# A fused attention and two-layer mixture kernel: a table of shifts on the due values of 426 planned tasks

## The chip, the core and the metric

The kernel runs on one core of one Trainium2 chip. A core has five engines, each with a queue of its own that runs in order: TensorE (PE in the rows) multiplies matrices, VectorE (DVE) and ScalarE (ACT) work on rows of up to 128 partitions, GpSimd (POOL) does a part of the elementwise work and the scattered writes, and SyncE (SP) starts most of the DMAs. An instruction that needs the result of another engine waits on a semaphore, and all that is queued behind it on its engine waits too. The metric is the device time of one launch in microseconds (us).

## The reference

```python
# 1. attention: 4 batches, 8 heads, 576 positions, 64 wide
scores = scale * np.matmul(q, k.transpose(0, 1, 3, 2))
mask = (rel >= 0) & (rel < 128)
scores = np.where(mask, scores + bias[None], -1000000000.0)
attn = np.exp(scores - np.max(scores, axis=-1, keepdims=True))
attn = attn / (np.sum(attn, axis=-1, keepdims=True) + 1e-09)
x = np.matmul(attn, v)              # to (2304 tokens, 512)
# 2. a dense layer
h = x @ w_in                        # 512 -> 2048
x = (h - np.tanh(h)) @ w_out        # 2048 -> 512
# 3. each token goes to the one best of 8 experts
logits = xn @ en.T / tau            # xn, en: normalised rows
expert_idx = np.argmax(logits, axis=1)
for e in range(8):
    h = np.maximum(x[mask] @ w1[e], 0.0)
    out[mask] = gate_w[mask, None] * (h @ w2[e])
```

All of it is in fp32. The kernel keeps that precision by splitting an operand into a high and a low part and adding three products (hi·hi, hi·lo, lo·hi); that is why one logical product is three matmuls, and why so many small casts and subtractions (`hi`, `lo`) go before each.

## The kernel before

The 2304 tokens are 18 blocks of 128 (`b`), and 9 groups of two blocks (`g`). The attention of a block goes in four quarters of two heads each (`quarter`, L479): scores on TensorE (L507 in the first four blocks, which are computed in plain fp32 on 64 of the array's rows per head, `jj` 0 on the upper half and 1 on the lower; L513 in the later blocks), bias and minimum on VectorE (`soft`, L520 to L535), the exponential on ScalarE (L549), a transpose (in the first blocks on TensorE, L570, with its copy out at L574), and the product with v (L584, later L595). `x_out` (L678) turns the block and splits it into `xT` (its low part at L700 on VectorE).

The dense layer goes in 72 steps `p`, eight for each group (`step`, L753): two groups of twelve matmuls into a bank `h` (L769; the bank alternates with `p % 2`), then tanh on ScalarE (L774), `h - tanh` on VectorE (L777), the split `gh` (ScalarE, L782) and `gl` (VectorE, L786), then four groups of three matmuls each that add to `acc` (L793). The 32 pieces of weight of this layer are loaded and split once, in the first 80 us, by `weight` (L338): `top`, `rest`, `hi`, `lo` (L354 to L366), on VectorE and ScalarE. `route` picks the expert of each token and scatters the rows into buckets (L951). Then follow eight experts with room for 384, 320, 320, 288, 288, 288, 288 and 256 tokens: `g1` (L1243) to a bank `he`, relu and split (L1259 on ScalarE, L1265 on VectorE), `g2` (L1278) to `y`, one tile of 128 tokens for each `t`, then a scale by the gate (L1299) and an indirect DMA from GpSimd that puts the rows into the result (L1303).

No engine's queue is written out by hand. Each piece of work is a task: `add` (L92) notes the engines that may do it with a cost in us on each, a `due` value (roughly the step in which it is wanted), and what it reads and writes. There are 3449 tasks, 969 of them TensorE's. `order` (L111) is a list scheduler over these costs: of all tasks that are ready it takes again and again the one with the least `(start, due, number)`, and gives it to the engine on which it ends first. `build` (L1398) then emits the tasks in that order, and each engine's queue is the tasks that it got. `due` thus decides between tasks that could start at the same planned time; and since VectorE or ScalarE, or VectorE or GpSimd, may do some of them, it decides the engine too.

Of the kernel before, what the change touches and what calls it, by code (L numbers as in the profile page):

```python
# [78 lines left out]
SPLIT = [i for i in range(NB) if (i * 128) % S > S - 128]  # L79


class Plan:


# [24 lines left out]
        self.tasks.append((eng, fn, due, deps, take, free, late, port, lag))  # L109

    def order(self, places):  # L111
        T = self.tasks
        nd = [len(t[3]) for t in T]
        out = [[] for _ in T]
        for n, t in enumerate(T):
            for d in t[3]:
                out[d].append(n)
        ready = [0.0] * len(T)
        free = {}
        pipe, pool = 0.0, (0.0, 0.0)  # L120
        avail = {p: [0.0] * c for p, c in places.items()}
        cand = [n for n in range(len(T)) if nd[n] == 0]
        res = []
        while cand:
            best = None
            now = min(max(ready[n], min(free.get(e, 0.0) for e in T[n][0])) for n in cand)
            load = {}
            for n in cand:
                eng = T[n][0]
                if len(eng) == 1 and ready[n] <= now + 1.0:  # L130
                    e, = eng
                    load[e] = load.get(e, 0.0) + eng[e]
            for n in cand:
# [10 lines left out]
                e = min(fin, key=fin.get)  # L144
# [1529 lines left out]
```

## Time and profile before

| | |
|---|---|
| median of 3 runs | 772.67 us (771.83 to 773.18) |
| profiled execution | 773.24 us, its span (first to last instruction) 771.4 us |
| granted TensorE clock, share of full speed | 0.999 |
| busy: TensorE, VectorE, ScalarE, GpSimd | 754.1, 547.3, 444.1, 324.1 us |
| share of the span | 98%, 71%, 58%, 42% |

The time that lies around the span is 773.24 - 771.4 = 1.84 us. A row of a timeline gives the start, the duration and the instruction with its line, out<-in, and how many instructions it joins; in brackets stands how long the engine was idle before it and what released it. Matmuls run in a pipeline, so the durations of two that follow one another overlap, and the price of a group is better read from one start to the next. A table of stretches gives the busy time of PE, PE's weight loads, DVE, ACT and POOL inside each stretch, with the instructions in brackets.

### The profile page before, as it was taken

The page shows a single profiled execution, that of the slowest core. Times are in us where ns is not written, and L with a number is a line of the kernel's source. Part 1 is how long each engine was busy: PE and PEld are TensorE (multiplying, and loading weights), DVE is VectorE, ACT ScalarE, POOL GpSimd, SP SyncE. Part 2 cuts the span into 40 slices and gives each one's busy share as a digit, 9 for nine tenths or more (in the row PEclk, how much of TensorE's full clock was granted, in tenths as well). Part 3 has the DMA queues.
Part 4 walks back from the last instruction along what each step waited for, and adds up shares of the span by engine and source line. Part 5 has one row for each costly group of instructions (what it writes and reads, how often), then busy time and mean ns, then how long its engine had stood idle before and what let it go on. Part 6 is the DMA issues. An engine that isn't in the chain of part 4 may idle for free.

```text
span 771.4 us, 15217 instructions
## 1 busy us (share of the span) xinstructions
PE 754.1 (98%) x5165; PEld 669.3 (87%) x5165; DVE 547.3 (71%) x1492; ACT 444.1 (58%) x1001; POOL 324.1 (42%) x340
## 2 busy tenths in 40 slices
PE   8999999999999999999999999999999999999996
PEld 5878899898989998999998998989889898898895
DVE  5789989878786778776787774787537786676420
ACT  5778876565666574675764743666245565565321
POOL 0052335867773465367474612412203531431211
PEclk9999999999999999999999999999999999999999
DMA  9994369947564564475465264474357989986100
GB/s 324 403 362 153 76 205 360 204 134 150 137 133 116 116 121 126 110 134 120 119 148 127 49 96 110 119 235 154 104 165 207 231 217 236 244 231 217 44 29 31
DMA packets 163734, 127.24 MB, mean 165 GB/s; under 512 B 126069, under 2 KB 130805, under 8 KB 163392
## 3 DMA queue, kind: packets, MB, share of 16 engines
q1 hardware_dynamic: 160336, 114.11, 56.9%
q0 software_dynamic: 3024, 11.82, 4.3%
q8 instruction: 42, 0.69, 0.4%
q14 instruction: 44, 0.36, 0.1%
q10 hardware_dynamic: 288, 0.26, 0.1%
HBM read 84.65 MB, written 22.06 MB: 138 GB/s over the span
## 4 chain that ended last, share of the span: by engine, by line
PE 78%; DVE 4%; issue 4%; POOL 2%; DMA 2%; ACT 1%; SPq 0%; POOLq 0%; ACTq 0%; DVEq 0%
PE h L769 24%; PE acc L793 23%; PE he L1243 10%; PE y L1278 9%; PE o L595 4%; PE sc L513 3%; PE y L1274 2%; DMA est<-in_w 2%; PE ht L1363 1%; PE misc L878 1%; POOL out L1303 1%; POOL bucket L951 1%; DVE sc L535 0%; DVE ph L559 0%; DVE eo L1141 0%
## 5 line engine op out<-in xcount | busy, mean ns | idle before, releaser
L769 PE MATMUL h<-xT,wi 128*128 128x256 f32 x1728 | 225.1, 284 | 0.9 <-DVE xT L730 0.6
L769 PEld LDWEIGHTS h<-xT,wi 128*128 128x128 f32 x1728 | 216.9, 191 | 7.0 <-DVE xT L730 0.9
L793 PE MATMUL acc<-wo,gh 128*128 128x512 f32 x576 | 182.2, 397 | 1.1 <-DVE wo L366 1.1
L793 PEld LDWEIGHTS acc<-wo,gh 128*128 128x128 f32 x576 | 100.9, 188 | 17.9 <-DVE wo L366 1.8
L793 PE MATMUL acc<-wo,gl 128*128 128x512 f32 x288 | 112.7, 391 | 0.0
L774 ACT ACTIVATE t<-h 128x512 f32<-128x512 f32 x72 | 43.0, 597 | 82.8 <-PE h L769 74.8
L1278 PE MATMUL y<-eo,ge 128*128 128x512 f32 x336 | 88.5, 398 | 1.0 <-ACT yo L1299 1.0
L549 ACT ACTIVATE p<-sc,mx 128x256 f32<-128x256 f32 (+1 forms) x128 | 58.9, 463 | 34.5 <-DVE mx L535 10.8
L559 POOL TENSOR_TENSOR ph<-p,ph 128x512 f16<-128x512 f32 (+1 forms) x40 | 47.0, 1175 | 63.7 <-ACT ph L554 47.6
L1278 PEld LDWEIGHTS y<-eo,ge 128*128 128x128 f32 x336 | 59.8, 188 | 11.3 <-ACT yo L1299 1.2
L786 DVE TENSOR_TENSOR gl<-t,gh 128x512 fp32r<-128x512 f32 x72 | 62.9, 874 | 3.4 <-ACT gh L782 2.9
L777 DVE TENSOR_TENSOR t<-h,t 128x512 f32<-128x512 f32 x72 | 49.4, 686 | 22.5 <-ACT t L774 22.2
L793 PEld LDWEIGHTS acc<-wo,gl 128*128 128x128 f32 x288 | 54.1, 188 | 12.7 <-DVE gl L786 0.8
L1265 DVE SCALAR_TENSOR_TENSOR ge<-he,ge 128x256 fp32r<-128x256 f32 x104 | 28.9, 316 | 50.6 <-ACT ge L1259 45.4
L535 DVE CUSTOM_DVE_ANT_0 sc<-sc,bias 128x256 f32<-128x256 f32 (+1 forms) x136 | 49.4, 374 | 21.2 <-PE sc L513 10.8
L400 POOL TENSOR_TENSOR khl<-stk,khl 64x512 fp32r<-64x512 f32 x30 | 40.2, 1339 | 55.8 <-ACT khl L396 50.6
L1259 ACT ACTIVATE ge<-he 128x288 fp32r<-128x288 f32 (+2 forms) x56 | 23.2, 415 | 66.0 <-PE he L1243 34.3
L1193 POOL TENSOR_TENSOR xf<-xe 128x512 f32<-128x512 bf16 (+2 forms) x19 | 21.0, 1107 | 90.4 <-DVE xT L1203 28.6
L1243 PEld LDWEIGHTS he<-xA,ei 128*128 128x128 f32 x384 | 54.3, 188 | 2.8
L1243 PE MATMUL he<-xA,ei 128*128 128x288 f32 (+2 forms) x384 | 56.1, 295 | 0.0
L1303 POOL DMA_INDIRECT out<-yo,ix x23 | 24.2, 1051 | 75.0 <-ACT yo L1299 70.8
L782 ACT CAST gh<-t 128x512 fp32r<-128x512 f32 x72 | 44.6, 620 | 19.0 <-DVE t L777 18.1
(227 smaller groups left out, 1429.8 us busy)
## 6 DMA issues: line engine op xcount, KB each, us to landing
est<-in_w SPq DMA_DIRECT2D x128, 256.0 KB
bucket<-in_c_pad SPq DMA_DIRECT2D x8, 1155.0 KB
rawi<-in_w_in SPq DMA_DIRECT2D x16, 511.8 KB
rawo<-in_w_out SPq DMA_DIRECT2D x16, 511.8 KB
stk<-in_k SPq DMA_DIRECT2D x30, 256.0 KB
stq<-in_q SPq DMA_DIRECT2D x28, 256.0 KB
vst<-in_v SPq DMA_DIRECT2D x30, 128.0 KB
xe<-bucket SPq DMA_DIRECT2D x3, 384.0 KB
```

Of the source, the lines that this page charges most:

```text
L400: self.eng(e).tensor_tensor(out=k, in0=r4("k")[64:128], in1=k.bitcast(F32), op=ALU.subtract)
L535: nc.vector.tensor_tensor_reduce(out=x, in0=x, in1=self.bias[:, h, c0:c1], scale=-0.125, scalar=mx[:, 1:2] if m else 3.0e38, op0=ALU.add, ...
L549: nc.scalar.activation(out=v["p32"][:, jj * W:(jj + 1) * W], in_=x, func=AF.Exp, scale=-1.0, bias=v["mx"][jj][:, 0:1], accum_out=self.sums ...
L559: self.eng(e).tensor_tensor(out=ph[:, 2 * W:4 * W], in0=v["p32"][:, 0:2 * W], in1=ph[:, 0:2 * W], op=ALU.subtract)
L769: nc.tensor.matmul(h3(v["h"], f2), lhsT=w[:, a, k, :], rhs=xT[c][:, :, k, :], start=(k == 0 and n == 0), stop=(k == KD - 1 and n == 2))
L774: nc.scalar.activation(out=v["t"], in_=v["h"].rearrange("p a b -> p (a b)"), func=AF.Tanh)
L777: nc.vector.tensor_tensor(out=v["t"], in0=v["h"].rearrange("p a b -> p (a b)"), in1=v["t"], op=ALU.subtract)
L782: nc.scalar.copy(out=v["gh"], in_=v["t"])
L786: self.eng(e).tensor_tensor(out=v["gl"], in0=v["t"], in1=v["gh"].bitcast(F32), op=ALU.subtract)
L793: nc.tensor.matmul(self.acc[g, t], lhsT=v[a][:, c0:c0 + 128], rhs=self.w["o", fs[f2]][:, c, :], start=(first and f2 == 0 and n == 0), stop ...
L1243: nc.tensor.matmul(h[:, 0:N], lhsT=w[:, a, c0:c0 + 128], rhs=xT()[b][:, k, 0:N], start=(k == 0 and n == 0), stop=(k == KD - 1 and n == 2))
L1278: nc.tensor.matmul(y[t], lhsT=gt(f, a)[:, (t - ts[0]) * 128:(t - ts[0] + 1) * 128], rhs=self.w["o", f0 + f][:, b, :], start=(f == 0 and n ...
```

## The change

A constant `SHIFT` gives for 426 task numbers a value that is added to the task's `due` before `order` starts; 325 of these tasks are TensorE's, 36 VectorE's, 33 ScalarE's, 24 SyncE's and 8 GpSimd's. The values go from -1545 to +271.5; negative ones put a task ahead of others that could start at the same planned time. A second table, `FIXED`, that could pin a task to an engine, is empty. No task is added or taken away and none does other work. Lines behind `order` stand 51 further down than before (L507 is L558, L793 is L844).

```diff
+SHIFT = {
+    9: 1.5, 28: 62.5, 38: -19, 48: -1, 82: 0.5, 95: -235.5, 96: -232, 102: -22, 105: -276.5, 106: -225.5, 112: -74.5,
...
+    -40.5, 3445: -34, 3446: -2,
+}
+FIXED = {}
 class Plan:
...
     def order(self, places):
-        T = self.tasks
+        T = list(self.tasks)
+        for n, d in SHIFT.items():
+            T[n] = T[n][:2] + (T[n][2] + d,) + T[n][3:]
+        for n, e in FIXED.items():
+            T[n] = ({e: T[n][0][e]},) + T[n][1:]
         nd = [len(t[3]) for t in T]
```

Of the 969 tasks on TensorE 754 stand at another place of its queue, by 3 places in the mean and 26 at most. 110 tasks change their engine: 33 go from ScalarE to VectorE and 33 the other way, 23 from GpSimd to VectorE and 21 the other way. On VectorE, twelve other tasks come ahead of the low part of `xT` of block 3 (L700, the last that the first dense groups wait for): three casts `hi` of weights, one `top`, one `rest`, three copies of transposed probabilities (L574), one `gl`, one low part of a key tile and two `soft`; five that stood ahead of it (three `top`, two L574) now stand behind it or are ScalarE's. On TensorE, two groups of L793 and two score groups more come ahead of the first matmul that reads that `xT`. The splits of the weight pieces `wo0`, `wi2` and `wi3` come earlier among VectorE's work. In the last three quarters of block 3, what stands on TensorE between the transposes (L570) and the product with v (L584) that needs their copy is now two score groups (before: one group of L769), one score group and two groups of L793 (before: two score groups), and one group each of L793 and L769 (before: one score group).

TensorE, the early attention at block 2 (`sc_97` is the bank of `jj` 0, `sc_98` that of `jj` 1, `kf` and `qf` are the keys and queries; L507 is scores, L570 a transpose, L584 the product with v, L689 the turn of a block), before:

```order
L584 MATMUL of<-vf_157,ptf 128x128 x4
L570 MATMUL misc<-con,p_315 128x128 x4
L507 MATMUL sc_97<-kf_178,qf_174 128x128
L507 MATMUL sc_97<-kf_142,qf_174 128x128
L507 MATMUL sc_98<-kf_178,qf_174 128x128
L507 MATMUL sc_98<-kf_142,qf_174 128x128
L570 MATMUL misc<-con,p32x 128x128 x4
```

and now, at the same place:

```order
L635 MATMUL of<-vf_156,ptf 128x128 x4
L558 MATMUL sc_97<-kf_176,qf_163 128x128
L558 MATMUL sc_97<-kf_142,qf_163 128x128
L740 MATMUL misc<-con,xr 128x128 x4
L635 MATMUL of<-vf_156,ptf 128x128 x4
L621 MATMUL misc<-con,p_314 128x128 x4
L621 MATMUL misc<-con,p32x 128x128 x4
L558 MATMUL sc_98<-kf_176,qf_163 128x128
L558 MATMUL sc_98<-kf_142,qf_163 128x128
L635 MATMUL of<-vf_156,ptf 128x128 x8
```

The two score groups of the two halves stood one behind the other; now the turn of block 0, a product with v and two transposes stand between them.

TensorE, the dense layer where step 50 begins (`h_5240` before, `h_5200` now, in the bank that step 48 used; `acc0` and `acc1` are the sums of the two token blocks), before:

```order
L513 MATMUL sc0_97<-khl_95,qst0_4863 128x256 x2
L513 MATMUL sc1_98<-khl_95,qst0_4863 128x256 x2
L793 MATMUL acc0_5209<-wo0_555,gh_5136 128x512 x2
L793 MATMUL acc0_5209<-wo0_555,gl_5144 128x512
L793 MATMUL acc1_5216<-wo0_555,gh_5136 128x512 x2
L793 MATMUL acc1_5216<-wo0_555,gl_5144 128x512
L793 MATMUL acc0_5209<-wo1_654,gh_5136 128x512 x2
L793 MATMUL acc0_5209<-wo1_654,gl_5144 128x512
L793 MATMUL acc1_5216<-wo1_654,gh_5136 128x512 x2
L793 MATMUL acc1_5216<-wo1_654,gl_5144 128x512
L769 MATMUL h_5240<-xT0_64,wi4_753 128x256
```

and now, where the group ahead is the second half of step 49 (`h_5114`), and ahead of that stand two score matmuls and then the end of step 48's own group in the same bank as `h_5200`:

```order
L820 MATMUL h_5133<-xT0_64,wi1_405 128x256
L564 MATMUL sc0_97<-khl_95,qst0_4954 128x256 x2
L820 MATMUL h_5114<-xT0_64,wi3_573 128x256
L820 MATMUL h_5114<-xT1_65,wi3_573 128x256
L820 MATMUL h_5114<-xT0_64,wi3_573 128x256 x2
L820 MATMUL h_5114<-xT1_65,wi3_573 128x256
L820 MATMUL h_5114<-xT0_64,wi3_573 128x256 x2
L820 MATMUL h_5114<-xT1_65,wi3_573 128x256
L820 MATMUL h_5114<-xT0_64,wi3_573 128x256 x2
L820 MATMUL h_5114<-xT1_65,wi3_573 128x256
L820 MATMUL h_5114<-xT0_64,wi3_573 128x256
L820 MATMUL h_5200<-xT0_64,wi4_791 128x256
```

Before, the four groups of L793 above, two score groups, a product with v and the two groups of step 49 stood between the last matmul into the bank and the next that overwrites it; now one group of twelve and two score matmuls do.

TensorE, the end of the program (the last expert's second product; `y_9891` and `y_9919` before, `y_9811` and `y_9818` now, are the two tiles of 128 tokens), before:

```order
L1278 MATMUL y_9891<-eo12_9448,gl4_9856 128x512 x3
L1278 MATMUL y_9891<-eo13_9473,gl5_9872 128x512 x3
L1278 MATMUL y_9891<-eo14_9514,gl6_9888 128x512 x3
L1278 MATMUL y_9891<-eo15_9577,gl7_9895 128x512 x3
L1278 MATMUL y_9919<-eo8_9307,gl0_9758 128x512 x3
L1278 MATMUL y_9919<-eo9_9375,gl1_9805 128x512 x3
L1278 MATMUL y_9919<-eo10_9409,gl2_9824 128x512 x3
L1278 MATMUL y_9919<-eo11_9434,gl3_9840 128x512 x3
L1278 MATMUL y_9919<-eo12_9448,gl4_9856 128x512 x3
L1278 MATMUL y_9919<-eo13_9473,gl5_9872 128x512 x3
L1278 MATMUL y_9919<-eo14_9514,gl6_9888 128x512 x3
L1278 MATMUL y_9919<-eo15_9577,gl7_9895 128x512 x3
```

and now:

```order
L1329 MATMUL y_9818<-eo13_9507,gl5_9860 128x512 x3
L1329 MATMUL y_9811<-eo13_9507,gl5_9860 128x512 x3
L1329 MATMUL y_9818<-eo14_9523,gl6_9926 128x512 x3
L1329 MATMUL y_9811<-eo14_9523,gl6_9926 128x512 x3
L1329 MATMUL y_9818<-eo15_9574,gl7_9904 128x512 x3
L1329 MATMUL y_9811<-eo15_9574,gl7_9904 128x512 x3
```

Before, one tile was finished with all its eight groups and then the other; now the two go side by side and end one group apart.

## Rows read from the trace of the kernel before

**Rows 1.** Page, first part: busy time by engine

```profile
PE 754.1 (98%) x5165; PEld 669.3 (87%) x5165; DVE 547.3 (71%) x1492; ACT 444.1 (58%) x1001; POOL 324.1 (42%) x340
```

**Rows 2.** Busy time by stretch: length, then busy us and instructions per engine, clock

```profile
10.00:45.00 35.00, 34.08 (x242) 27.25 (x241) 26.02 (x94) 25.63 (x72) 6.59 (x11) 1.00 1.03 399
45.00:80.00 35.00, 32.49 (x229) 28.51 (x228) 32.93 (x70) 29.90 (x64) 10.95 (x11) 1.00 0.63 216
...
110.00:530.00 420.00, 417.19 (x3099) 377.16 (x3098) 320.76 (x912) 252.75 (x592) 224.12 (x221) 1.00 0.61 146
530.00:740.00 210.00, 207.79 (x1225) 183.97 (x1224) 132.48 (x331) 102.43 (x201) 64.48 (x59) 1.00 0.65 174
```

**Rows 3.** Waits of PE: released by, us in total, times, longest

```profile
PE of L584 <- ACT ptf L574: 2.0, 3, 0.9
PE sc L513 <- ACT p L549: 1.7, 3, 0.6
...
PE acc L793 <- DVE wo L366: 1.1, 2, 0.7
```

**Rows 4.** Timeline of PE, early scores: start, us, instruction, count

```profile
16.44 0.48 PE L507 MATMUL sc<-kf,qf 64*128 64x256 f32 x1
16.44 0.48 PE L507 MATMUL scx<-kf,qf 64*128 64x256 f32 x1
...
17.07 0.66 PE L689 MATMUL misc<-con,xr 128*128 128x128 f32 x4
...
18.99 0.70 PE L507 MATMUL scx<-kf,qf 64*128 64x256 f32 x2
19.61 1.16 PE L584 MATMUL of<-vf,ptf 128*128 128x128 f32 x8
```

**Rows 5.** Timeline of PE, 53 to 64 us

```profile
53.65 1.16 PE L584 MATMUL of<-vf,ptf 128*128 128x128 f32 x8 [0.59 <-ACT ptf L574]
...
59.03 1.16 PE L584 MATMUL of<-vf,ptf 128*128 128x128 f32 x8 [0.50 <-ACT ptf L574]
...
61.68 0.63 PE L793 MATMUL acc<-wo,gh 128*128 128x512 f32 x2
...
62.38 0.39 PE L513 MATMUL sc<-khl,qst 128*128 128x256 f32 x2
62.61 1.60 PE L769 MATMUL h<-xT,wi 128*128 128x256 f32 x12
```

**Rows 6.** Timeline of DVE, a cast, and the last early xT

```profile
48.59 0.46 DVE L354 CAST x3T<-rawo 128x512 f16<-128x512 bf16 x1
...
65.86 0.68 DVE L700 TENSOR_TENSOR xT<-misc,xT 128x512 fp32r<-128x512 f32 x1
```

**Rows 7.** Lines of the first step engine work: ns minimum, median, maximum

```profile
L786 DVE TENSOR_TENSOR gl<-t,gh x72: 670/692/1693, 35.0 to 527.3; 128x512 fp32r<-128x512 f32 x72
...
L777 DVE TENSOR_TENSOR t<-h,t x72: 660/687/693, 33.6 to 525.2; 128x512 f32<-128x512 f32 x72
...
L774 ACT ACTIVATE t<-h x72: 587/597/602, 32.9 to 524.6; 128x512 f32<-128x512 f32 x72
```

**Rows 8.** Timeline of all engines, 304 to 309 us

```profile
305.85 1.35 POOL L408 TENSOR_TENSOR qst<-stq,qst 128x512 fp32r<-128x512 f32 x1
305.97 1.77 DVE L559 TENSOR_TENSOR ph<-p,ph 128x512 f16<-128x512 f32 x1
...
308.49 0.47 PE L513 MATMUL sc<-khl,qst 128*128 128x256 f32 x2 [0.62 <-ACT p L549]
```

**Rows 9.** Timeline of the last expert

```profile
743.70 0.99 POOL L1303 DMA_INDIRECT out<-yo,ix  x1 [23.75 <-ACT yo L1299]
...
744.99 0.99 POOL L1303 DMA_INDIRECT out<-yo,ix  x1 [0.30 <-issue]
...
764.88 0.69 ACT L1299 ACTIVATE yo<-y,ga 128x512 f32<-128x512 f32 x1 [4.70 <-PE y L1278]
765.84 0.98 POOL L1303 DMA_INDIRECT out<-yo,ix  x1 [4.40 <-ACT yo L1299]
```

40 rows, old and new, of the table SHIFT are left out of this document.

## The prediction

> **What bounds the kernel now.** I read the busy time by engine first: TensorE works 754.1 of 771.4 us [rows 1], and the change gives it the same matmuls, so that the only time to be won is the 17.3 us in which it is idle. The stretches say where these lie [rows 2]: 0.92 us in 10 to 45, 2.51 in 45 to 80, 2.81 in the 420 us from 110 to 530, 2.21 in the 210 us from 530 to 740; what is left, some 9 us, lies before 10 us (first loads, warming) and behind the last matmul. The granted clock is 1.00 in all of them, so nothing here is a matter of clock. Third, TensorE's waits [rows 3]: the copy of the transposed probabilities (`ptf`, 2.0 us in 3 places), exponentials (1.7 in 3), a split of `wo` (1.1 in 2). So the kernel is a TensorE queue with a few holes of 0.4 to 1 us, each at one place where another engine's result came late. A new order can close holes or open them. It can also change two things that are no holes: how matmuls overlap on TensorE, and what follows the last matmul.
>
> **Part 1: score groups that lose their partner.** In the first blocks the scores of the two halves use 64 rows of the array each. Where a group of one half follows a group of the other, both start at once, at 16.44, and the next instruction starts at 17.07: 0.63 us for two. A group alone, at 18.99, has its successor at 19.61: 0.62 us for one [rows 4]. A pair torn apart thus costs one group more, 0.62. Nine such neighbours stand in the queue before and five after. Two of the five that go (the first block, before 10 us, where TensorE waits for loads anyway) are made up for by one that is new; of the other four each costs 0.62, which is 2.5 us. The place shown at block 2 is one of them. In 10 to 45 us TensorE is busy 34.08 of 35 [rows 2], so there is hardly a hole there that could swallow it; in 45 to 80 there are 2.51 us of holes, and of these the waits on VectorE's `wo`, 1.1 [rows 3], would shrink when TensorE comes later (waits in a chain that TensorE itself starts, as for `ptf`, would not). I take 2.5 - 1.1 = 1.4; the bounds are 0 (all swallowed) and 2.5.
>
> The Trainium skill, "TensorEngine Tiling (Array Packing)", Key Properties, says that different tiles run in parallel, and also that a change of the tiling mode drains TensorE. The first half is what the row at 16.44 shows; the second would put a price on each change from a 64-row score to a full-size matmul, of which the new order has more. The row at 18.99 holds that price already, since the group alone is followed by full-size work: by the rule and by the row the sum is the same 0.62 for each pair.
>
> **Part 2: the front, up to the `xT` of block 3.** Two holes close. The products with v at 53.65 and 59.03 waited 0.59 and 0.50 for their `ptf` [rows 5]. The prices of what stands in between are read from one start to the next: a group of L793 0.70 (61.68 to 62.38), a score group of the later kind 0.23 (62.38 to 62.61), and a group of L769, busy 1.60 and overlapped at its end by 0.16 as the score group is (0.39 against 0.23), 1.44 [rows 5]. Now two L793 groups and a score stand between the first product and its transposes, 1.6 us, and an L793 and an L769 group before the second, 2.1: both holes close, -1.1. One place gets worse: the second quarter of block 3 had an L769 group there, 1.44, and now has two score groups, one of each kind, 0.62 + 0.23 = 0.85. The copy came 0.50 late behind a single score group of 0.23 and 0.59 late behind two early ones, so I put 0.3 there. Against this stands VectorE. TensorE's first reader of block 3's `xT` comes right behind the subtraction at 65.86 [rows 6]. Ahead of that subtraction now stand twelve more VectorE tasks: five of about 0.69, and seven casts, copies and `soft` of 0.46 to 0.7, say 0.55 [rows 6], 7.3 us; five of about 0.5 have gone, 2.5. TensorE's own additional work ahead of the reader is two L793 groups and two scores, 2 x 0.70 + 2 x 0.23 = 1.9. That is 4.8 - 1.9 = 2.9 us by which VectorE falls behind, if it had no idle time. But it had 9.0 us of it in 10 to 45 [rows 2], and several of the twelve (the splits of `wo0`, `wi2`, `wi3`) are pulled into that time; in 45 to 80 it had 2.1. The 9.0 is three times the 2.9, so I take 0 for this, bounds 0 and +2.9, and below nothing the two `wo` waits, which may go with the earlier splits, -1.1. Part 2: -1.1 + 0.3 = -0.8, from -2.2 to +2.4.
>
> **Part 3: the dense layer, 110 to 530 us.** Before, TensorE's queue had slack nearly everywhere: I followed, for each TensorE task, the chain of ScalarE and VectorE work from the last TensorE task that it hangs on, and compared it with TensorE's own work between the two. Under 0.6 us to spare I count 3 places before and 22 after; under 1 us, 7 and 52. Step 50 is one of them. The bank is free again after a tanh, 0.60, and a subtraction, 0.69 [rows 7], and two handoffs, some 0.3 in all: 1.59 us; what stands between now is a group of L769 and a score group, 1.44 + 0.23 = 1.67 [rows 5]. It fits by 0.08, so long as VectorE starts at once and nothing on it is long. VectorE is sometimes long: `gl` takes 692 ns as a rule, but up to 1693 [rows 7], and at 305.97 a `ph` took 1.77 us beside a GpSimd instruction begun at 305.85, after which the score at 308.49 came 0.62 late [rows 8]. With a mean for `gl` of 62.9/72 = 874 ns, the share of the long ones is about (874 - 692)/1000, 0.18. A place with 0.3 us to spare then loses 0.7, one with 0.8 loses 0.2: 22 x 0.18 x 0.7 + 30 x 0.18 x 0.2 = 3.9, against 3 x 0.18 x 0.7 + 4 x 0.18 x 0.2 = 0.5 by the same count before. That is an estimate of +3.4; against it I set half of the 2.81 us of old holes [rows 2], since their instructions have other neighbours now: -1.4. Part 3: +2.0. Bounds: all old holes gone and none new, -2.8; the long instruction at each of the 22, 22 x 0.7 less 2.8, +12.6. The taken value lies near the row of before, where the five holes of such a size made up the whole 2.81.
>
> The Trainium skill, "SBUF — State Buffer", in its section on two separate sides, says that VectorE and GpSimd share a pair of ports, and that the one that comes second blocks until the other's whole instruction is done. The rows at 305.85 and 305.97 agree. A planner that keeps VectorE off the port for that time, as `order` does only for the tasks marked `port`, would by the rule pay nothing; that the long ones are still in the trace says that it doesn't catch them all.
>
> **Part 4: the experts and the end.** In the experts the same count goes from 5 places under 0.6 us to about 20, but GpSimd is busy only 64 of 210 us there, against 224 of 420 in the dense layer [rows 2], and several of the 2.21 us of holes may go; 0, bounds -2.2 (all their holes) and +2.5 (20 places x 0.18 x 0.7). At the end, TensorE's stop releases ScalarE's scale at 764.88, and GpSimd puts at 765.84, 0.96 behind the scale's start [rows 9]. Two puts that both are ready start 1.29 apart (743.70, 744.99) [rows 9]. Now one tile ends one group, 0.70, before TensorE stops, and the other with it: the first put can start 0.30 after the stop, the second 1.29 later, at 1.59, where the last one started 1.00 after the stop before. +0.6, bounds 0 and +1.3.
>
> **The sum.** 1.4 - 0.8 + 2.0 + 0.6 = +3.2 us on the profiled execution's 773.24, 776.4. That execution is 0.57 above the median of 772.67, so a median of 775.9 answers to it.
>
> **The rivals.** (a) *The holes close.* A hole is a place where TensorE had too little work between handing a bank on and needing the answer; more work put there closes it. The places are those of rows 3 and the five of the dense layer: 2.81 us there, 1.1 at the two `ptf`, 1.1 at the two `wo`, 5.0 in all, and with +0.6 at the end the time is 772.67 - 5.0 + 0.6 = 768.3. For it: at the two `ptf` the plain count of work in between says so. Against: the spare time between producer and consumer falls nearly everywhere else. It decides, as faster by more than 1.55 us, so long as new holes and torn pairs cost under 5.0 - 0.6 - 1.55 = 2.85 us. (b) *Nothing that can be told.* TensorE's 754.1 us stay; holes closed and opened cancel, as -2.8 and +3.4 in part 3 nearly do, and the torn pairs and the end cancel against part 2. About 772.7. By 0.2%, 1.55 us, a measurement of this kernel can be told from no change, so this case goes from 771.1 to 774.2. (c) *VectorE falls behind in the front.* The 2.9 us come in full, at the first reader of block 3's `xT`, with the torn pairs in full as far as they come before it, and the tight places of part 3 as taken: 772.67 + 2.9 + 1.4 + 2.0 + 0.6 - 0.8 = 778.8. Against it are the 9.0 us of idle time. That the table does nothing is no case: 754 of 969 TensorE tasks stand elsewhere.
>
> **How the numbers follow.** The forecast, slower by tight places, torn pairs and the end, 0.36, with a range of its own from 774.2 to 777.5; (c) 0.08; (b) 0.20; (a) 0.36, from 766 to 771. Slower is 0.44, same 0.20, faster 0.36. Leaving out half of what (c) may reach and the lower end of (a), the range is 767.0 to 779.0.
>
> **What the new profile would show.** Part 1: a lone `sc` at block 2 with 0.6 us to its successor, and TensorE's busy time up by about 2 us. Part 2: no wait at the two products with v, a short one in the second quarter, and VectorE's last early `xT` no later than TensorE's reader by more than before. Part 3: the idle time of TensorE in 110 to 530 up from 2.81 to about 5, in waits of a `h` or `acc` matmul for a VectorE instruction that took over 1 us. Part 4: the two last puts 1.3 us apart, the last 1.6 behind TensorE's stop. The prediction is wrong if idle time in the dense layer falls, or if the front ends sooner than before.

## The result, and the profile after

The changed kernel takes 781.19 us in the median of 4 runs (779.38 to 785.41), beside 772.92 (771.83 to 774.29) for the one before on the same chip: a ratio of 1.0114, 95% interval 1.0070 to 1.0158. It is slower, as forecast, but by 8.3 us and not by 3; the time lies above the range of 767.0 to 779.0.

The profiled execution is the longest of the four, 785.41, with a span of 783.6. The page of the kernel after, busy time by engine:

```profile
PE 761.1 (97%) x5165; PEld 671.3 (86%) x5165; DVE 545.5 (70%) x1494; ACT 443.4 (57%) x1001; POOL 328.1 (42%) x338
```

TensorE's busy time is 7.0 us above that of [rows 1] with the same matmuls. So part of the loss is no wait: the same work took longer. The stretches of [rows 2], after:

```profile
10.00:45.00 35.00, 34.34 (x226) 27.79 (x226) 24.62 (x81) 24.50 (x67) 6.07 (x9) 0.95 0.99 378
...
110.00:530.00 420.00, 415.89 (x3074) 374.89 (x3073) 315.77 (x892) 249.89 (x587) 221.76 (x216) 1.00 0.59 142
530.00:740.00 210.00, 204.35 (x1198) 178.95 (x1197) 137.58 (x346) 105.81 (x206) 67.73 (x62) 1.00 0.69 184
```

TensorE's idle time goes from 2.81 to 4.11 us in 110 to 530, and from 2.21 to 5.65 in the experts. In 10 to 45 the clock is 0.95 in the mean. TensorE's waits, after (the answer to [rows 3]: released by, us in total, times, longest):

```profile
PE sc L564 <- ACT p L600: 3.4, 3, 2.3
PE y L1329 <- ACT ge L1310: 2.5, 2, 1.9
...
PE acc L844 <- DVE gl L837: 0.9, 2, 0.7
```

The waits for `ptf` are gone from the top; there are a few long waits instead, and only 0.9 us in waits for `gl`, on which part 3 rested.

To place the loss I gave each matmul its median distance to the next start in the trace before, summed these along TensorE's queue, and compared at equal sums when the two kernels get there. This is called the progress below (us behind before, in the profiled executions; for after they sum to 11.0 of the 12.2 by which the spans differ, the rest lies in the end):

| piece of the program (TensorE work done) | after | `c_khl` | `c_all` | `x_front` | `mix` |
|---|---|---|---|---|---|
| front, up to 75 us | +3.6 | +1.5 | +3.5 | +0.7 | +0.2 |
| dense layer, 75 to 385 | +0.5 | +0.4 | +0.4 | +0.1 | -1.6 |
| one place, 385 to 410 | **+2.9** | 0.0 | -0.1 | -0.1 | 0.0 |
| on to 600 | -0.6 | -0.7 | -0.5 | +0.2 | -0.6 |
| experts, 600 to 680 | **+4.5** | +3.0 | +3.5 | +0.2 | -0.9 |
| to the last matmul | +0.1 | +0.1 | 0.0 | 0.0 | 0.0 |

The new order loses in three pieces, which are read one by one. The columns behind `after` belong to kernels of the next section.

One profile stands behind each column, so the entries have their own noise. `b_khl`, `w_rev` and `l_rev` below have the order before in 75 to 385, and by the same sums they stand 0.8 to 1.1 ahead of before there; `mix` has the order before in the experts and shows -0.9; `after` and `c_khl` have one and the same order in the experts and differ by 1.5. An entry of about 1 us is thus no price by itself.

**The place at 420 us.** Timelines of GpSimd, ScalarE and TensorE, after (start, us, engine, instruction; in brackets the idle time before it and its releaser):

```profile
415.26 0.96 POOL L1002 DMA_INDIRECT bucket<-xrow,ix  x1 [0.18 <-issue]
419.92 1.29 POOL L451 TENSOR_TENSOR khl<-stk,khl 64x512 fp32r<-64x512 f32 x1 [3.70 <-DMA bucket<-xrow,ix]
421.30 0.62 POOL L679 TENSOR_TENSOR xr<-xr,sm 128x256 f32<-128x256 f32 x1
...
422.49 1.33 POOL L610 TENSOR_TENSOR ph<-p,ph 128x512 f16<-128x512 f32 x1
...
423.86 0.47 ACT L600 ACTIVATE p<-sc,mx 128x256 f32<-128x256 f32 x1 [0.39 <-POOL ph L610]
...
424.48 0.50 PE L564 MATMUL sc<-khl,qst 128*128 128x256 f32 x2 [2.28 <-ACT p L600]
424.82 2.75 PE L820 MATMUL h<-xT,wi 128*128 128x256 f32 x12
```

The low part of a key tile (`khl`) waits 3.70 us until the scatter issued ahead of it has landed. Behind it on GpSimd stand the product `xr`, a low part of v (`vst`) and the low part `ph` of the exponentials; ScalarE's next `p` starts behind `ph`, and the scores of TensorE wait for that `p`: 2.28 us. The twelve matmuls behind it take 2.75 us, against 1.60 in [rows 5]. The stretches say why:

```profile
422.00:424.00 2.00, 0.20 (x4) 0.02 (x1) 2.00 (x2) 1.04 (x3) 2.00 (x3) 1.00 0.39 131
424.00:426.00 2.00, 1.52 (x8) 1.52 (x9) 2.00 (x6) 1.91 (x6) 1.90 (x3) 0.73 0.52 98
426.00:428.00 2.00, 2.00 (x11) 2.00 (x11) 0.43 (x1) 0.60 (x1) 1.45 (x1) 0.50 1.06 188
428.00:430.00 2.00, 2.00 (x16) 1.91 (x15) 1.90 (x5) 1.96 (x5) 0.00 (x0) 0.92 0.87 233
```

The granted clock falls from 2.4 to 1.2 GHz (0.50) behind the wait. Before, GpSimd's order is another:

```profile
410.11 0.96 POOL L951 DMA_INDIRECT bucket<-xrow,ix  x1 [0.18 <-issue]
411.84 0.61 POOL L628 TENSOR_TENSOR xr<-xr,sm 128x256 f32<-128x256 f32 x1 [0.77 <-DVE xr L614]
412.51 0.94 POOL L472 TENSOR_TENSOR vst<-vst,vt 128x256 f32<-128x256 f32 x1
413.86 1.69 POOL L400 TENSOR_TENSOR khl<-stk,khl 64x512 fp32r<-64x512 f32 x1 [0.41 <-ACT khl L396]
```

There `khl` starts 3.75 us behind the scatter, released by ScalarE's cast of the high part, but two urgent instructions stand in between. TensorE's score behind this place, at 418.61, waits 0.61 us, and the clock stays at 1.00.

**The experts, 635 to 657 us.** SyncE's queue, VectorE, ScalarE and TensorE after:

```profile
639.02 7.57 SPq L1226 DMA_TRANSPOSE xe<-bucket  x2
646.85 1.09 SPq L1184 DMA_DIRECT2D est<-in_w  x2
...
648.04 0.15 DVE L1238 CAST ix<-side 128x1 int32<-128x1 f32 x1 [5.38 <-DMA out<-yo,ix]
...
652.62 1.31 ACT L1188 CAST eo<-est 128x512 fp32r<-128x512 f32 x2 [7.91 <-DMA est<-in_w]
...
649.18 1.21 PE L1329 MATMUL y<-eo,ge 128*128 128x512 f32 x4 [1.24 <-DVE ge L1316]
...
654.29 0.97 PE L1329 MATMUL y<-eo,ge 128*128 128x512 f32 x3 [1.85 <-ACT ge L1310]
```

Two transposing loads hold SyncE's queue for 7.57 us; the two loads of weights behind them (`est`) start at 646.85, and ScalarE stands 7.91 us at the cast that needs them, with the relus for TensorE queued behind it. Of the 7.91 us, 5.8 lie between the start of the first of these loads and the cast. VectorE stands 5.38 us until an output put has landed. Before, two loads of weights stood between the two transposing loads:

```profile
635.08 3.59 SPq L1175 DMA_TRANSPOSE xe<-bucket  x1
638.94 0.56 SPq L1131 DMA_DIRECT2D est<-in_w  x1
639.75 0.60 SPq L1133 DMA_DIRECT2D est<-in_w  x1
640.55 1.82 SPq L1175 DMA_TRANSPOSE xe<-bucket  x1
```

**The front.** TensorE, after, and the clock in the 1 us stretches from 10:

```profile
10.66 0.68 PE L635 MATMUL of<-vf,ptf 128*128 128x128 f32 x4 [1.89 <-DMA vf<-in_v]
...
17.82 0.70 PE L558 MATMUL sc<-kf,qf 64*128 64x256 f32 x2
18.45 0.71 PE L635 MATMUL of<-vf,ptf 128*128 128x128 f32 x4
...
56.83 1.05 PE L635 MATMUL of<-vf,ptf 128*128 128x128 f32 x8
...
60.38 1.05 PE L635 MATMUL of<-vf,ptf 128*128 128x128 f32 x8
```

```profile
11.00:12.00 1.00, 1.00 (x9) 0.71 (x8) 0.21 (x1) 0.00 (x0) 0.00 (x0) 0.96 1.00 395
12.00:13.00 1.00, 1.00 (x6) 0.17 (x3) 0.15 (x2) 0.37 (x1) 0.00 (x0) 0.50 1.07 414
```

A score group without its partner stands at 17.82, with 0.63 us to its successor, the price of [rows 4]; the products at 56.83 and 60.38 no longer wait, as [rows 5] was to change. The wait for `vf` with its clock fall (0.50 up to 15 us) is no fixed part of the order: `x_exp` below, which has the order before up to 515 us, shows the same (1.6 us, then 0.50), while `x_front` and `c_khl`, with the new front, waited 0.3 and lost no clock. Whether the new order makes it more frequent is not shown.

**The end.** After:

```profile
771.57 4.27 PE L1329 MATMUL y<-eo,gl 128*128 128x512 f32 x18
...
776.21 0.98 POOL L1354 DMA_INDIRECT out<-yo,ix  x1 [17.39 <-ACT yo L1350]
777.49 0.99 POOL L1354 DMA_INDIRECT out<-yo,ix  x1 [0.30 <-issue]
```

The puts start 1.28 apart, and the last 1.65 behind TensorE's stop at 775.84, where [rows 9] give 1.00.

### The profile page after: what moved, and what is told of

Read it like the earlier page. It is cut to its first block, busy times and chain, and to the rows that moved or that the text cites. A ratio compares the mean times of both kernels' runs of the same rounds, so it can differ in the third digit from the quotient of the medians.

```text
span 783.6 us, 15228 instructions
## 1 busy us (share of the span) xinstructions
PE 761.1 (97%) x5165; PEld 671.3 (86%) x5165; DVE 545.5 (70%) x1494; ACT 443.4 (57%) x1001; POOL 328.1 (42%) x338
## 4 chain that ended last, share of the span: by engine, by line
PE 79%; issue 8%; DVE 3%; POOL 3%; DMA 3%; ACT 2%; SPq 2%; POOLq 0%; ACTq 0%; DVEq 0%
PE h L820 25%; PE acc L844 24%; PE he L1294 8%; PE y L1329 7%; PE o L646 3%; PE sc L564 3%; PE y L1325 2%; DMA est<-in_w 2%; PE of L635 1%; PE sc L558 1%; POOL out L1354 1%; PE misc L621 1%; DMA vf<-in_v 1%; PE ht L1414 1%; POOL ph L610 1%
## 5 line engine op out<-in xcount | busy, mean ns | idle before, releaser
L820 PE MATMUL h<-xT,wi 128*128 128x256 f32 x1728 | 229.4, 285 | 0.1
L844 PE MATMUL acc<-wo,gh 128*128 128x512 f32 x576 | 183.1, 399 | 0.3 <-DVE wo L417 0.3
L844 PE MATMUL acc<-wo,gl 128*128 128x512 f32 x288 | 113.0, 392 | 0.9 <-DVE gl L837 0.9
L844 PEld LDWEIGHTS acc<-wo,gh 128*128 128x128 f32 x576 | 99.7, 189 | 15.4 <-DVE wo L417 0.9
L610 POOL TENSOR_TENSOR ph<-p,ph 128x512 f16<-128x512 f32 (+1 forms) x51 | 64.1, 1257 | 55.3 <-ACT ph L605 25.3
L837 DVE TENSOR_TENSOR gl<-t,gh 128x512 fp32r<-128x512 f32 x72 | 65.0, 903 | 5.5 <-ACT gh L833 5.0
L844 PEld LDWEIGHTS acc<-wo,gl 128*128 128x128 f32 x288 | 54.1, 188 | 14.1 <-DVE gl L837 2.2
L1192 DVE TENSOR_TENSOR eo<-est,eo 128x512 fp32r<-128x512 f32 x64 | 50.3, 795 | 8.2 <-ACT eo L1188 8.1
L1294 PEld LDWEIGHTS he<-xT,ei 128*128 128x128 f32 x384 | 53.9, 188 | 2.4
L1294 PE MATMUL he<-xT,ei 128*128 128x288 f32 (+2 forms) x384 | 55.4, 295 | 0.0
L451 POOL TENSOR_TENSOR khl<-stk,khl 64x512 fp32r<-64x512 f32 x23 | 31.1, 1352 | 57.1 <-DMA rawi<-in_w_in 30.9
```

The lines of the kernel that those rows point to most:

```text
L610: self.eng(e).tensor_tensor(out=ph[:, 2 * W:4 * W], in0=v["p32"][:, 0:2 * W], in1=ph[:, 0:2 * W], op=ALU.subtract)
L820: nc.tensor.matmul(h3(v["h"], f2), lhsT=w[:, a, k, :], rhs=xT[c][:, :, k, :], start=(k == 0 and n == 0), stop=(k == KD - 1 and n == 2))
L837: self.eng(e).tensor_tensor(out=v["gl"], in0=v["t"], in1=v["gh"].bitcast(F32), op=ALU.subtract)
L844: nc.tensor.matmul(self.acc[g, t], lhsT=v[a][:, c0:c0 + 128], rhs=self.w["o", fs[f2]][:, c, :], start=(first and f2 == 0 and n == 0), stop ...
L1192: self.eng(eng).tensor_tensor(out=t[:, 1, :], in0=v["x"], in1=t[:, 0, :].bitcast(F32), op=ALU.subtract)
L1294: nc.tensor.matmul(h[:, 0:N], lhsT=w[:, a, c0:c0 + 128], rhs=xT()[b][:, k, 0:N], start=(k == 0 and n == 0), stop=(k == KD - 1 and n == 2))
```

## The experiments

The kernels below hold the order of the 3449 tasks and their engines as a list (`PLAN`), so that any piece of either order can be put into the other; their lines stand 62 further down than those of after. Each was timed in five rounds beside the kernel before, which had medians of 772.3 to 773.2.

**Four pieces of the order apart.** Each is the order before with one piece of the order after:

```diff
-PLAN = before
+x_front: PLAN = after[:351], then what is left of before
+x_dense: PLAN = before[:347], after up to 2415, then before
+x_exp:   PLAN = before[:2414], after up to 3368, then before
+x_tail:  PLAN = before[:3368], then after
```

> The new order for the first 351 planned tasks (to about 75 us), the old order for all the rest. Theory one (a few places: TensorE waits 1.9 us for the first piece of v at 10 us and its clock then falls to half speed until 15 us): 3 to 4 us slower than before, some 776, with granted clock below 1 near 12 us in the profile. Theory two (as predicted: torn pairs of scores and tight places, spread out): about 0.6 us slower, 773.5, clock 1.00.

> The old order up to about 75 us, the new order from there to the first expert (about 517 us), then the old order again. Theory one: 2 us slower, as -1.2 up to 400 us and +3.3 at one stall near 420 us, with the clock falling behind that stall. Theory two: 2 us slower too, but in many waits of 0.3 to 0.7 us and with the clock at 1.00.

> The old order up to the first expert, the new order for the experts but the last, the old order for the last. Theory one (VectorE stands at the index cast of a tile until the put of an earlier expert has landed, and the splits behind it are late): 4.5 us slower, 777.2, in two stalls near 640 us. Theory two: no difference that can be measured.

> The old order except for the last 81 planned tasks (the last expert's second product), which come in the new order: the two tiles side by side. Both theories: 0.6 us slower, the last two puts 1.3 us apart.

| | median (range), runs | ratio, 95% interval |
|---|---|---|
| `x_front` | 774.23 (771.67 to 780.80), 12 | 1.0036 (1.0010 to 1.0062) |
| `x_dense` | 780.33 (779.74 to 780.86), 4 | 1.0095 (1.0075 to 1.0115) |
| `x_exp` | 776.64 (773.61 to 780.61), 7 | 1.0052 (1.0027 to 1.0077) |
| `x_tail` | 774.48 (772.74 to 777.64, and one run at 1038.34 that the ratio leaves out), 12 | 1.0019 (1.0001 to 1.0036) |

The four medians lie 13 us above before in sum, more than after's 8.3, since seams cost: by the progress `x_dense` loses 2.4 us where it leaves the order before (waits for a split of `wi` and for an exponential, 1.0 us each, and for a split of `wo`, 0.7) and 2.8 where it returns; in between, from 75 to 480 us of work, it loses 2.6, and so does after. `x_exp` in its profile lost 1.9 in the front, which is the order before, and 1.5 in 580 to 680. Its interval therefore is no price of the experts' order. From here the pieces are judged by the progress, and the medians only where the front does not decide.

**The place at 420 us, undone in after and done in before.** GpSimd's queue in `c_khl`, against after, and in `b_khl`, against before:

```diff
 L1064 DMA bucket<-xrow_91,ix 18688x770
-L513 TENSOR_TENSOR khl<-stk,khl 64x512
 L741 TENSOR_TENSOR xr<-xr,sm 128x256
 L585 TENSOR_TENSOR vst_5315<-vst_5315,vt 128x256
+L513 TENSOR_TENSOR khl<-stk,khl 64x512
...
 L1064 DMA bucket<-xrow_91,ix 18688x770
+L513 TENSOR_TENSOR khl<-stk,khl 64x512
 L741 TENSOR_TENSOR xr<-xr,sm 128x256
 L585 TENSOR_TENSOR vst_5345<-vst_5345,vt 128x256
-L513 TENSOR_TENSOR khl<-stk,khl 64x512
```

In `b_khl` VectorE's copy `x<-xr` moves as well, behind three instructions of VectorE; in `c_khl` no other queue changes.

> The new order with one instruction of GpSimd moved: the low part of a key tile behind the scatter near 420 us goes behind the two short instructions that stood behind it (a product of rows of the attention with the row sums, and a low part of v), as in the old order. Theory one (a few places): the 2.3 us stall of TensorE at 422 us and the low clock behind it go, 3.3 us faster than the new order, some 778. Theory two (spread out): no difference that can be measured, 781.

> The old order with the same change made the other way: near 420 us the low part of the key tile goes ahead of the two short GpSimd instructions. Theory one: a stall of 1.5 to 2.5 us appears there that the old order does not have, and with it perhaps a stretch at the low clock: 2 to 3.5 us slower than before, 775 to 776.5. Theory two: no difference that can be measured.

`c_khl`: 778.48 (775.39 to 780.45, 9 runs), ratio 1.0071 (1.0048 to 1.0094), 2.7 below after, whose interval (from 1.0070) it overlaps. Its GpSimd and TensorE at the place:

```profile
413.08 0.96 POOL L1064 DMA_INDIRECT bucket<-xrow,ix  x1 [0.18 <-issue]
415.34 0.61 POOL L741 TENSOR_TENSOR xr<-xr,sm 128x256 f32<-128x256 f32 x1 [1.30 <-DVE xr L727]
...
417.73 1.29 POOL L513 TENSOR_TENSOR khl<-stk,khl 64x512 fp32r<-64x512 f32 x1 [1.02 <-DMA bucket<-xrow,ix]
...
420.90 0.50 PE L626 MATMUL sc<-khl,qst 128*128 128x256 f32 x2 [0.89 <-ACT p L662]
```

`khl` starts as late (4.65 us from the scatter's start, 4.66 in after), but `xr` is past it; TensorE waits 0.89 and its clock stays at 1.00. The piece goes from +2.9 to 0.0. `b_khl`: 775.33 (771.72 to 781.22, 12 runs), ratio 1.0026 (1.0003 to 1.0049); its profile loses 3.4 us at the place, with this row and this stretch:

```profile
419.51 0.47 PE L626 MATMUL sc<-khl,qst 128*128 128x256 f32 x2 [2.46 <-ACT p L662]
```

```profile
420.00:422.00 2.00, 2.00 (x6) 1.51 (x6) 1.21 (x5) 1.45 (x4) 0.96 (x1) 0.50 1.10 193
```

One GpSimd instruction moved past two others thus changes the time by about 3 us in either direction: 2.9 and 3.4 by the progress, 2.7 and 2.2 by the medians, with the wait and the clock fall coming and going with it. This is shown. The other profiles with the new order at this place have the wait too (2.17 us in `x_dense`, 2.28 in `c_keep`, 2.33 in `c_act`). That the landing is what holds `khl` is read from after and `c_khl`; in `b_khl` the scatter landed at 412.24 and `khl` started at 412.92, just behind ScalarE's cast of the high part (412.15 to 412.77).

**The experts: who stands first.** `c_keep` moves the cast of `ix` that waits for the put; `c_act` also the cast from `est` on ScalarE; `c_all` has both, `khl` put back, and the last expert in the order before:

```diff
 c_keep: PLAN = after, but
-  keep(3018) ahead of the splits; its next load (3142)
+  keep(3018), load(3142) ahead of task 3025, behind the splits
 c_act: c_keep, but
+  hi(2883) behind relu(2937), lo(2884) behind 2938, load(2977) behind it
 c_all: c_act and c_khl, the last 81 tasks as before
```

> The new order with one instruction of VectorE moved: the cast of the row numbers of the fifth expert's first tile, which waits for a put to land, goes from 642 us to behind the splits that stand behind it, where the old order has it. Theory one: the waits of TensorE at 649 and 654 us (1.2 and 1.9 us) go, 3 us faster than the new order, some 778. Theory two: no difference. A third outcome, the first wait gone and the second not, would say that the second is the weights' own loads.

> The new order with the index cast moved as before and, on ScalarE, the cast of one piece of the fourth expert's weights (its load lies behind two slow transposing loads in SyncE's queue) moved from in front of two relu casts to behind them, with its subtraction and the load that needs its buffer. Theory one (an engine's queue stands behind one instruction that waits for a DMA): both waits near 650 us go, 4 us faster than the new order, some 777. Rival (the loads themselves are late, whoever waits first): the wait only moves to the matmul that reads the piece, and the time stays at 781.

> The new order with all three repairs: the key tile behind the two short GpSimd instructions, the two casts of the experts behind the splits, and the last expert in the old order. Theory one (these places are all that the new order costs, but for the front): 3.0 + 4 + 0.7 us faster than the new order, 773 to 774, no difference from before that can be measured. Theory two (a spread cost of tight places remains): 776 or more.

| | median (range), runs | ratio, 95% interval | lost in 600 to 680 us of work |
|---|---|---|---|
| `c_keep` | 782.46 (780.48 to 786.45), 6 | 1.0121 (1.0087 to 1.0154) | +4.3 |
| `c_act` | 782.07 (779.94 to 787.25), 6 | 1.0116 (1.0091 to 1.0141) | +6.3 |
| `c_all` | 779.88 (778.23 to 781.63), 6 | 1.0086 (1.0066 to 1.0106) | +3.5 |

My theory that the two long waits are the price, each to be moved out of the way, fell: neither `c_keep` nor `c_act` is faster than after's 781.19, and `c_all` came to 779.88 where 773 to 774 was expected, which is what the theory of a spread cost foretold (776 or more). In `c_keep` VectorE's wait is gone and ScalarE's is 7.38; in `c_act` ScalarE stands 8.08 at a cast from `est`. TensorE waits 2.95 and 2.84 us there, and the clock falls behind both waits, which is in their +4.3 and +6.3. TensorE in `c_keep`:

```profile
651.86 0.97 PE L1391 MATMUL y<-eo,ge 128*128 128x512 f32 x3 [2.95 <-ACT ge L1372]
...
653.39 2.77 PE L1391 MATMUL y<-eo,ge 128*128 128x512 f32 x6
```

Its granted clock is 0.50 from 654 to 656 us, and the six matmuls at 653.39 take 2.77 us where six take 1.67 in `w_all` (644.96, below).

`c_all` has the order of `c_act` at this place, and in its profile ScalarE stands 5.68 us and TensorE only 0.44:

```profile
648.13 0.97 PE L1391 MATMUL y<-eo,ge 128*128 128x512 f32 x3 [0.44 <-ACT ge L1372]
```

The length of this wait is thus not set by the order alone, and no single profile gives its price.

**The experts: what comes late.** The subtraction 2848 that frees one of the six `est` buffers stands 21.7 us of TensorE's work later than before, and with it every later load into this buffer. `w_exp` and `w_all` put these 22 tasks back (into `x_exp`, and into after with `khl` and the last expert put back); `w_rev` gives only their delay to before. `l_all` and `l_rev` do the same with all 405 tasks of the loading side between 545 and 690 us of work:

```diff
-PLAN = base
+PLAN = base, the named tasks (22 or 405) at the place in TensorE's work
+       that the other order gives them; all other tasks keep their order
```

> x_exp, that is before with the order after only in the experts 0 to 6, but with the 22 tasks of one weight buffer (the load, cast and subtraction of `est` buffer 1, from the subtraction 2848 on: loads 2864, 2882, 2977, 2995, 3013, 3108, 3126) put back to where TensorE's queue stands in the order before. In x_exp these stand 12 to 22 us of TensorE's work later than before, all others within 7. If that one chain, begun by the late subtraction 2848, is what makes the weights late: the +3.5 of x_exp against before goes to about 0 to +1, so 773 to 774 us, the lag at 640 to 680 us falls from about 2.5 to under 1, and ScalarE's waits for `est` between 600 and 680 fall to about 5 us. If the lateness is spread over all the experts (other moved tasks): no change from x_exp, 776 to 777. A run that meets the clock fall at 12 us is 1.6 longer in either case.

> After, with three pieces put back: the low part of the key (khl) behind the product and the transposes at 420 us as in c_khl, the chain of weight buffer 1 as in w_exp, and the last expert in the order before. If the two places and the end are what the new order cost, 0 to -1 against before stays besides the front: 772 to 775 us, some 7 below after; c_all, which left the chain late, had 779.9. If the chain is not it: 779 to 780, as c_all.

> Before, with only the 22 tasks of weight buffer 1 put to where TensorE's queue stands in the order after, 12 to 22 us of TensorE's work later. If the chain is the cause by itself: +2 to +5, 775 to 778 us, with ScalarE waiting over 5 us at a cast from `est` near 640 to 655 and TensorE behind it. If it needs the rest of the new order beside it (transposing loads ahead on SyncE, the products pulled early): under +1, 773 us.

> After with khl put back as in c_khl, the last expert in the order before, and, in the experts from 545 to 690 us of TensorE's work, all 405 tasks of the loading side (the weights' loads, casts and subtractions; the rows' transposing and side loads, joins, splits and casts of ix) put where TensorE's queue stands in the order before; the products, relus and outputs stay in the new order. If the loading side as a whole is what was late: the progress against before between 580 and 680 us, which lost 3.5 in c_all and 2.5 with one weight buffer put back (w_all), loses under 1, and the profile comes out at 773 to 775 us by itself (or as far above as its front is). If the products' order is the cause: still 2.5 or more.

> Before, with only those 405 tasks of the loading side put to where TensorE's queue stands in the order after. If the loading side alone makes the loss: +2 to +4 between 580 and 680 us, 775 to 777 us, with casts on ScalarE or VectorE that wait 4 us or more. If it needs the products' new order: within 1 of before.

| | median (range), runs | ratio, 95% interval | lost in 580 to 680 us of work |
|---|---|---|---|
| `w_exp` | 776.75 (774.78 to 778.27), 8 | 1.0047 (1.0029 to 1.0066) | +0.5 (`x_exp` +1.5) |
| `w_all` | 778.58 (775.49 to 783.39), 10 | 1.0078 (1.0054 to 1.0103) | +2.5 (`c_all` +3.4) |
| `w_rev` | 772.44 (771.58 to 775.27), 12 | 1.0001 (0.9983 to 1.0019) | -0.7 |
| `l_all` | 776.98 (775.81 to 777.60), 7 | 1.0047 (1.0029 to 1.0064) | +1.8 |
| `l_rev` | 777.52 (776.99 to 779.19), 6 | 1.0064 (1.0045 to 1.0084) | +3.9 |

By the progress the one buffer is worth 0.9 to 1.0 us in both surroundings, which is no more than two profiles of one order differ by; by the medians `w_exp` is no better than `x_exp` (776.64), and the intervals of `w_all` and `c_all` overlap. By itself it is worth nothing: `w_rev` missed the +2 to +5. So no price of this buffer is shown. In `w_all` two transposing loads still stand on SyncE with one load of weights between them, and ScalarE still stands long:

```profile
643.98 0.62 ACT L1250 CAST eo<-est 128x512 fp32r<-128x512 f32 x1 [5.11 <-DMA est<-in_w]
...
644.96 1.67 PE L1391 MATMUL y<-eo,ge 128*128 128x512 f32 x6 [1.24 <-ACT ge L1372]
```

With the whole loading side back (`l_all`) the loss in this stretch is 1.8, in waits of TensorE each under 1 us at four places, and the interval lies below that of `c_all` (1.0066 to 1.0106), though not below that of `c_khl` (1.0048 to 1.0094), whose experts lost 3.0. ScalarE's longest wait for `est` (the answer by releaser, as in [rows 3]) still ends near 645 us, and TensorE's wait behind it is as short as in `c_all`:

```profile
ACT ei L1250 <- DMA est<-in_w: 10.7, 9, 4.6
...
649.63 1.11 PE L1391 MATMUL y<-eo,ge 128*128 128x512 f32 x3 [0.53 <-ACT ge L1372]
```

The other way round (`l_rev`) the loss comes all at once and elsewhere, at one output:

```profile
693.20 1.22 PE L1387 MATMUL y<-eo,ge 128*128 128x512 f32 x2 [2.36 <-DVE yo L1403]
```

```profile
694.00:696.00 2.00, 2.00 (x9) 1.90 (x9) 1.38 (x4) 0.49 (x1) 1.91 (x3) 0.50 0.69 245
```

The casts that should have waited 4 us or more in `l_rev` did not (3.3 at most). What is shown: the new order of the loading side alone makes the kernel before slower, by a ratio of 1.0064. Taking it out of the new order leaves 1.8 of 3.0 to 3.4 us, a difference not much above that of two profiles of one order. That the rest is a mismatch of loads and products taken from two orders is a guess. Which of the 405 tasks matter stays open; no run moved the transposing loads by themselves.

`w_exp` has one more thing in its profile: its median is no better than that of `x_exp`, for its front, which is the order before, lost 4.2 us. TensorE there at 14.40, where the kernel before has 0.60 us for the same pair of instructions at 11.49:

```profile
14.40 1.03 PE L368 MATMUL misc<-fill 128*128 128x512 bf16 x2
```

**The good pieces.** `mix` is before with the order after in two stretches, about 146 to 245 and 480 to 550 us, where the progress of after wins. `f_pairs` is `x_front` with three torn score pairs joined again; `mix2` is that front and the two stretches:

```diff
-PLAN = before
+mix:  PLAN = before[:689], after up to 1221, before up to 2313, after up to 2595, before
-x_front: scores 126, 243, 146 apart from their partners
+f_pairs: 126 behind 172, 243 behind 242, 146 behind 296
+mix2: f_pairs' first 351 tasks, then mix
```

> The old order, but the new one in two stretches, about 146 to 245 us and 480 to 550 us, in which the new profile gained on the old (1.3 and 0.9 us). Theory one (places, each by itself): 1.5 to 2 us faster than before, 771. Theory two (what is gained is given back further on by tight places): no difference that can be measured.

> The new order of the front (first 351 tasks) with three of the torn pairs of score groups put side by side again, the old order for the rest. If a torn pair costs 0.6 us and nothing hides it: 1.9 us faster than the front in the new order as it was, about 771 to 772 in the undisturbed runs. If VectorE or the loads bound the front anyway: no difference from that.

> The front with the pairs put together again, and the two stretches of the new order that gained (146 to 245 and 480 to 550 us), the old order for all the rest. If the gains add: 2 us of the two stretches and about 1 of the front, 769.5 to 770.5. If the front gives nothing: 771, as with the two stretches alone.

`mix`: 771.32 (769.98 to 772.67, 12 runs), ratio 0.9976 (0.9962 to 0.9991), the one kernel here whose interval lies below 1. In its profile the dense layer is

```profile
110.00:530.00 420.00, 418.44 (x3110) 378.99 (x3109) 314.18 (x910) 254.19 (x597) 219.07 (x218) 1.00 0.61 144
```

with 1.56 us of idle time where [rows 2] have 2.81. Not all of its progress is its own: some 0.8 of the -1.6 fall near 300 us and the -0.9 in the experts, where its order is that before. `f_pairs`: 773.08 (771.76 to 775.42, 12 runs), ratio 1.0008 (0.9996 to 1.0020), against 1.0036 for `x_front`; by the progress at 75 us it is 0.8 us earlier. The intervals of `f_pairs` and `x_front` overlap; TensorE's busy time falls from 756.9 to 755.4 us. `mix2`: 771.16 (769.90 to 776.18, 12 runs), ratio 0.9982 (0.9961 to 1.0003), no better than `mix`.

## Why the prediction was right and wrong

The sign was right, and its reasons were right in part; the size was wrong by 5 us. `c_khl` was profiled in an execution at its median; with its rows and the 2.9 us of the one place, the loss is 1.5 in the front, 2.6 in the dense layer, 3.1 in the experts and 1.0 in the end, 8.2 in all, against the 8.3 of the medians. The prediction had 0.6, 2.0, 0 and 0.6. The experts are 3 of the 5 us.

- **Part 1, the torn pairs (+1.4).** Right in the mechanism, near in size. A lone group costs 0.63 (17.82), as taken. TensorE's busy time is up by 2.8 us in `x_front`, where about 2 was foretold, and joining three torn pairs takes 1.5 of that away; in the progress it gives back 0.8, where three quarters of the 1.4 are 1.1.
- **Part 2, the front (-0.8).** Right in its steps: the two waits for `ptf` are gone, and no wait of TensorE for VectorE's late `xT` shows. Its upper bound of +2.4 does not add up: -1.1 + 0.3 + 2.9 is 2.1. Parts 1 and 2 together were +0.6; `x_front` is at +0.7 in 75 us of work, after without its clock fall (`c_khl`) at +1.5. The fall at 12 us was not in the sum: a run of either order can have it.
- **Part 3, the dense layer (+2.0).** The size came out near, +2.8 (0.5 + 2.9 - 0.6), by luck: the mechanism fell. The 22 places with under 0.6 us to spare, and the 3.4 us drawn from them, cost next to nothing: waits for `gl` are 0.9 us, and outside the one place the layer is level with before. The 2.9 us come from a row that the count did not see, a GpSimd instruction that waits for a DMA to land. The count followed chains from one matmul through ScalarE and VectorE to the next; a chain that begins at a landing was not in it.
- **Part 4, the experts (0, at most +2.5).** This is the step that failed: 4.5 us in the profiled execution, 3.0 in `c_khl`. I argued from tight places and from GpSimd's low share of busy time, and put the term at nothing. In its place the profile of after has waits of TensorE for relus (`ge`), 2.5 and 1.4 us, while ScalarE stands 7.91 us at a cast of weights that have not landed. The order of the loading side, which no count followed, costs time by itself: put alone into the kernel before, a ratio of 1.0064 (`l_rev`), though at another place. That the transposing loads on SyncE ahead of the weights are the reason in after is argued, not shown, and the cause of most of the 3.0 to 4.5 us stays open. SyncE's order was not read, though 24 of the shifted tasks are SyncE's.
- **The end (+0.6).** Right in mechanism: the last put 0.65 us later behind TensorE's stop. `x_tail` has 1.0019, some 1.5 us, with an interval that holds 0.6.
- **Left out of the sum:** that a wait is paid twice. At 420 us TensorE waits 2.28 and then runs at half clock for about 3 us, which is some 1.5 us more.

Of the rivals, (c) had the nearest number, 778.8, for a reason that did not come true: VectorE did not fall behind in the front. (a) needed the holes to close without new ones: the two at `ptf` did, and of the 1.1 us for splits of `wo` 0.3 is left, but new waits came.

## What to carry to other kernels

When a new order is judged, follow the instructions that wait for a DMA to land, on every queue, and read SyncE's order too: what stood behind one such instruction cost 2.9 us here, while 22 chains with under 0.6 us to spare cost next to nothing. Price a long wait of TensorE with the half-speed stretch that may follow, read from the granted clock. And an order is not all good or bad: cut it in pieces, keep those that win, and judge a piece by its progress inside a profile where something outside it, here the first 17 us, moves the median. First find out how far two profiles of one order differ: here that was 1 us and more.

## What the runs showed of the hardware

- The granted clock fell to 0.50 behind waits of TensorE of 2.28 us (after, 424 us), 2.46 (`b_khl`), 2.36 (`l_rev`), 2.95 (`c_keep`), 2.84 (`c_act`), 1.89 (after, 10.66 us) and 1.59 (`x_exp`, 10.05 us). It did not fall behind the wait of 0.89 in `c_khl`, nor behind the 1.85 us in after's experts (654.29). A wait of such a length is thus sometimes paid with half speed and sometimes not.
- In `w_exp` the stretches give the clock as 1.00 from 6 to 18 us, while its matmuls took 1.7 times as long as in the kernel before up to 17 us. There the durations say more than the granted clock.
